# Loads of v and z on another queue, with casts on two engines, and two more blocks taken from their transposes

## The chip, the core and the metric

The kernel runs on one core of a Trainium2 chip. The metric is the device time of one execution in microseconds (us); lower is better. The core has TensorE (PE, matmuls), VectorE (DVE), ScalarE (ACT), GpSimd (POOL) and SyncE (SP), which here does nothing but issue transfers, and 16 DMA engines that move the data of all queues.

## What is computed

For each of 8 batches, with S = 3200 rows, D = 256, and z 64 wide:

```
scores = z @ z.T / S                       # symmetric, S x S
x      = u * (max(scores, 0)**2 @ v)       # S x D
q, k   = x @ w_q, x @ w_k                  # S x 64
mixed  = (q @ k.T / 8) @ x                 # done as q @ (k.T @ x)
out    = max(mixed, 0) @ w_out             # float32
```

Inputs and output are float32; the kernel's matmuls run in float16, but for a few at the end.

## The kernel before

The 3200 rows of a batch are 25 row tiles of 128. Columns are worked on in seven groups, six of 512 and one of 128 (`widths`, `starts`; `LASTG` is the last). One *score tile* is (batch, group gi, row tile ti): 128 rows by the group's columns.

*First product.* `scores` makes two score tiles at once (a pair), one on each half of PE's rows, line L263. `first_stage` takes max(., 0) and scales into a tile `g`, on ACT (L286) or DVE (L290). `second_stage` squares `g` into a float16 tile `at`, on ACT (L306) or POOL (L308). There are 16 buffers of `at` (`NAT`) and 7 of `g`.

*Turned blocks.* The scores are symmetric, so the block (gi, gj) transposed is the block (gj, gi). Where `is_turned` says so (gi < gj, and gj at most `FAR` = 2 groups on or the last group), the second one is not computed: `turn` sends the first one's `at` tiles through a transposing transfer of SP's queue (L330) into one of `NHOME` = 7 homes (`tt`, or `ttl` for the last group). Batch 0 leaves one such block out (`SKIP`).

*Second product.* For each group, `second_product` (L351) accumulates `at` (or `tt`, `ttl`) times `v` over the 25 row tiles in PSUM (`acc`), in two halves. `gate` takes the result out (L368, L369) and multiplies it by u into x on POOL (L388).

*The token part.* x is transposed by SP's queue (L400), projected to q and k (L417), the keys are transposed by SP's queue (L436) and doubled on POOL (L448), k.T @ x is summed up (L455, L470), and after the last group of a batch the mixing (L483) and the output projection (L521) run in the next batch's time, with stores on SP's queue (L552).

*v and z of the next batch.* `load_v` (L150) and `load_z` (L156) are transfers of POOL's queue that convert float32 to float16 on the way: z in one, v in five of 5 row tiles. `turn_z` (L163) then transposes z by SP's queue into `zT`. u is loaded by SP's queue (L174) as float32.

*The order of the work* is fixed when the program is written, by a planner that keeps a clock for each engine, and for SP's queue and the DMA engines (`sp_at`, `dma_at`). `move(ready, due, issue, takes, fn, landed, may)` registers a transfer of SP's queue; `send` issues the one that is due first once it is ready and calls `landed` with the time at which the data is reckoned to be there. `at_time` runs something at a time. `use_pair` makes a pair of score tiles, `squares` places second stages, `acc_step` issues second products, `half_done` gates, `use_keys`, `use_heads`, `use_mix` and `use_projs` the token part. The plan's times only set the order; on the chip each instruction waits for what it really needs, and each engine and queue keeps its order.

Of the kernel before, what the change touches and what calls it, by code (L numbers as in the profile page):

```python
# [16 lines left out]
def kernel(  # L17
# [45 lines left out]
    pk = ctx.enter_context(tc.tile_pool(name="pk", bufs=3))  # L63
    pxt = ctx.enter_context(tc.tile_pool(name="pxt", bufs=NXT))
    pu = ctx.enter_context(tc.tile_pool(name="pu", bufs=2))
    pg = ctx.enter_context(tc.tile_pool(name="pg", bufs=7))
    psum = ctx.enter_context(tc.tile_pool(name="psum", bufs=3))
    pat = ctx.enter_context(tc.tile_pool(name="pat", bufs=NAT))
    ptt = ctx.enter_context(tc.tile_pool(name="ptt", bufs=1))
# [20 lines left out]
    def rows(t, b):  # L90
        return t[b].rearrange("(p n) d -> p n d", n=NT)
# [52 lines left out]
            nc.tensor.matmul(out=idle[:, 0:P], lhsT=blank, rhs=blank, start=True, stop=True)  # L144
        clock[PE] += 0.053 * cold() * n

    def load_v(b, n0, nn):
        if n0 == 0:
            vs[b] = pv.tile([P, NT, D], FP16, tag="v_sb", name="v_sb")
        nc.gpsimd.dma_start(out=vs[b][:, n0 : n0 + nn, :], in_=rows(v, b)[:, n0 : n0 + nn, :])  # L150

    ztimes = []
    ZTURNS = [(0, 0, 7), (1, 0, 7), (0, 7, 13), (1, 7, 13)]

    def load_z(b):
        nc.gpsimd.dma_start(out=zn[:, 1 : NT + 1, :], in_=rows(z, b))  # L156

    def turn_z(b, i):
        odd, m0, m1 = ZTURNS[i]
# [48 lines left out]


    SKIP = [(0, 2)]  # L210
    EXTRA = []

    def is_turned(b, gi, gj):
        if b == 0 and (gi, gj) in SKIP:
# [392 lines left out]
    moves = []  # L607
    sp_at, dma_at = [0.0], [0.0]
    LANDS = 4.0
    RING = 2.0  # L610
    SLACK = 1.0

    def at_time(t, fn):
        later.append((t, fn))

    def move(ready, due, issue, takes, fn, landed=None, may=None):
        moves.append((ready, due, issue, takes, fn, landed, may))

# [36 lines left out]

    FARDUE = 12.0
    SPLIT = 0.2
    UNTIL = 24.0

    def choose(a, d):  # L660
        t = shut() + LATE
# [33 lines left out]
    def squares():  # L695
        while pending and pending[0][0] <= clock[PE] + 0.3:
            ready, p, g = pending.pop(0)
            a, c = max(clock[ACT], ready), max(clock[POOL], ready)
            by_act = a + SPARE < c and (a + 1.06 <= shut() + LATE or a + 2.5 < c)
            ways = [by_act]  # L700
            if clock[PE] < UNTIL and max(a + 0.63, c + 1.05) + SPLIT < min(a + 1.06, c + 1.9):
                ways = [a < c, a >= c]
                done = max(give(ACT, ready, 0.63), give(POOL, ready, 1.05))
            else:
                done = give(ACT, ready, 1.06) if by_act else give(POOL, ready, 1.9)
            for (b, gi, gj, _, nn, _, _), turn in second_stage(p, g, ways):
# [24 lines left out]

    def use_keys(b, gi):
        open_slot()
        ps = ps_tile("qk")
        prior = None
        if keyed and keys_at.get(keyed[0], 1e9) <= clock[PE]:
            prior = keyed.pop(0)
        projections(b, gi, ps, stop=not prior)
        clock[PE] += 0.44 if gi < LASTG else 0.24
        if prior:  # L740
            heads(*prior, ps, halves(gi))
            clock[PE] += 0.44 if prior[1] < LASTG else 0.11
        ready = clock[PE] + FROM_PE
        a, d = (max(clock[x], ready) for x in (ACT, DVE))
        by_act = a + 0.58 <= d + 0.69 or d + 0.69 > shut() + LATE + 0.6
        projections_out(b, gi, ps, by_act)
        done = give(ACT, ready, 0.58) if by_act else give(DVE, ready, 0.69)
        n = widths[gi] / P
        final = (b, gi) == (last, LASTG - 2)
        if not final:  # L750
            move(
                done + SLACK, done + 10.0, 1.28, 0.21 * n, lambda: turn_keys(b, gi),
                lambda t: at_time(t, lambda: double(b, gi)),
            )
            keyed.append((b, gi))
        if prior:
            heads_out(*prior, ps)
            done = give(DVE, done, 0.7)
            if prior[1] == LASTG:
                give(POOL, done, 0.6)  # L760
                heads_known(prior[0])
        close_slot(done)
        if len(keyed) == 2 and gi == LASTG:
            add_extra(done + 14.0, "heads", use_heads)
        if final:
            for _ in keyed[1:]:
                add_extra(done, "heads", use_heads)
# [49 lines left out]
    def project_out(b, gi, ps, ready):  # L817
        stores = []
        on_act = max(clock[ACT], ready) + BIAS <= max(clock[DVE], ready) + 0.2
        proj_out(b, gi, ps, [(not on_act, nc.sync, widths[gi] // P)], stores)  # L820
        engine, t = (ACT, 1.0) if on_act else (DVE, 1.23)
        done = give(engine, ready, t if gi < LASTG else 0.3)
        close_slot(done)
        i = len(stored)
        if gi < LASTG:
            stored.append(1e9)

        def landed(t):
# [12 lines left out]
    V1 = 10  # L841

    def batch_begun(b, t):
        if b + 1 < B:
            t0 = max(t + 6, Z0)
            at_time(t0, lambda: (load_z(b + 1), push(3.0)))
            step = ZSTEP if b else ZSTEP0
            for i, (_, m0, m1) in enumerate(ZTURNS):
                move(
                    t0 + ZWAIT + step * i, t0 + ZDUE + step * i, 1.28, 0.21 * (m1 - m0),  # L850
                    lambda i=i: turn_z(b + 1, i),
                    lambda t, i=i: z_ready.update({(b + 1, i): t}),
                )
# [4 lines left out]
    def v_loaded(b, n0, nn):  # L858
        load_v(b, n0, nn)
        push(2.5)  # L860
        for n in range(n0, n0 + nn):
            v_at[b, n] = dma_at[0] + 5.0

    z_ready = {}

# [4 lines left out]
    def group_begun(b, gi, t):  # L870
        if gi == 0:
            batch_begun(b, t)
        if gi + 1 < NG:
            move(max(t + 2, clock[POOL] + SLACK), t + 7, 0.55, 1.6, lambda: load_u(b, gi + 1))
        elif b + 1 < B:
            move(max(t + 2, clock[POOL] + SLACK), t + 7, 0.55, 1.6, lambda: load_u(b + 1, 0))

    SPARE = 0.5
    BIAS = 0.2
    XDUE = 5.0  # L880
    XWAIT = 2.0
    LATE = 0.5

    def half_done(b, gi, half):
# [10 lines left out]
        if half == halves(gi)[-1]:  # L895
            n = 8 if widths[gi] == W else 2
            move(
                t + SLACK, t + XDUE, 1.28, 0.21 * n, lambda: turn_x(b, gi),
                lambda t: x_landed(t, b, gi), lambda: len(xTs) < NXT,
            )  # L900

# [119 lines left out]
    move(10.0, 14.0, 0.55, 1.6, lambda: load_u(0, 0))  # L1021
# [153 lines left out]
```

## Time and profile before

| | |
|---|---|
| median of 3 runs | 775.03 us (774.68 to 778.61) |
| profiled execution | 773.15 us, its span 770.9 us |
| granted TensorE clock in it | 0.997 |
| queue of SP (hardware) | 300224 packets, 123.13 MB |
| queue of POOL (software) | 6624 packets, 15.98 MB |
| score matmuls (L263) | 924 |
| second-product matmuls (L351) | 10000 |
| transposing transfers of tt / ttl / x / keys / z | 143 / 48 / 56 / 53 / 28 |

The span is what lies between the first and the last recorded instruction; the execution's own time is 2.25 us longer. Busy times are unions of an engine's instructions; a line such as L263 is a line of the kernel before. "A <- B" after a wait means that A waited and that B ended the wait.

### The profile page before, as it was taken

How to read it: one execution, taken by the hardware profiler on the slowest of the kernel's cores; microseconds unless marked ns; L12 is line 12 of the kernel's file. 1: busy time of each engine (PE TensorE's matmuls, PEld its weight loads, DVE VectorE, ACT ScalarE, POOL GpSimd, SP SyncE). 2: the span in 40 equal slices, each digit the busy share in tenths (PEclk: the TensorE clock that was granted, in tenths of full speed). 3: DMA queues.
4: the chain of work that ended last, by engine and by line, in shares of the span. 5: the costliest groups of instructions: out<-in, count | busy, mean ns of one | idle time of the engine just before them, and what ended most of it. 6: DMA issues, size and time to landing. Idle time of an engine off the chain costs nothing.

```text
span 770.9 us, 28221 instructions
## 1 busy us (share of the span) xinstructions
PE 761.7 (99%) x12408; PEld 678.4 (88%) x12408; DVE 510.5 (66%) x537; ACT 561.2 (73%) x647; POOL 591.1 (77%) x496
## 2 busy tenths in 40 slices
PE   8999999999999999999999999999999999999996
PEld 7889998888898888989889988998889989898884
DVE  6775876675787566765677756765667476675645
ACT  7785876778758678875788677877777676777734
POOL 8796788789687778666778687887878887888740
PEclk9999999999999999999999999999999999999998
DMA  8999999999999999999899999999999998979625
GB/s 199 130 187 182 167 204 173 160 212 194 194 162 189 194 209 190 182 213 203 153 190 162 188 231 163 219 145 160 262 156 192 184 190 211 201 143 203 152 84 191
DMA packets 307114, 141.09 MB, mean 183 GB/s; under 512 B 285744, under 2 KB 288432, under 8 KB 306992
## 3 DMA queue, kind: packets, MB, share of 16 engines
q1 hardware_dynamic: 300224, 123.13, 85.0%
q0 software_dynamic: 6624, 15.98, 14.8%
q8 instruction: 97, 1.59, 0.9%
q14 instruction: 25, 0.20, 0.1%
q10 hardware_dynamic: 144, 0.20, 0.1%
HBM read 59.64 MB, written 26.21 MB: 111 GB/s over the span
## 4 chain that ended last, share of the span: by engine, by line
PE 94%; POOL 2%; DVE 1%; DMA 1%; ACT 1%; issue 1%; POOLq 0%; SPq 0%; DVEq 0%; ACTq 0%
PE acc L351 68%; PE sc L263 13%; PE fo L521 6%; PE qk L417 3%; PE qk L455 2%; POOL at L308 2%; PE mx L483 1%; DMA z<-in_z_dram 1%; POOL x_sb L388 1%; DVE g L290 0%; ACT g L286 0%; DVE fo L546 0%; DMA xT_sb<-x_sb 0%; PE hd L455 0%; ACT at L306 0%
## 5 line engine op out<-in xcount | busy, mean ns | idle before, releaser
L351 PE MATMUL acc<-v_sb,at 64*128 64x256 f16 x7344 | 504.7, 269 | 0.0
L308 POOL TENSOR_TENSOR at<-g 128x1024 f16<-128x1024 f32 (+1 forms) x218 | 402.3, 1859 | 71.6 <-ACT g L286 29.1
L351 PEld LDWEIGHTS <-at 64*128 64x128 f16 x7344 | 407.2, 94 | 48.1 <-issue 4.8
L290 DVE TENSOR_SCALAR g<-sc 128x1024 f32<-128x1024 f32 (+2 forms) x285 | 338.5, 1203 | 122.8 <-PE sc L263 114.3
L306 ACT ACTIVATE at<-g 128x1024 f16<-128x1024 f32 (+2 forms) x255 | 257.2, 1023 | 21.8 <-DVE g L290 17.8
L286 ACT ACTIVATE g<-sc 128x1024 f32<-128x1024 f32 (+2 forms) x186 | 183.2, 989 | 76.8 <-PE sc L263 75.0
L388 POOL TENSOR_TENSOR x_sb<-both,u_sb 128x512 f16<-128x512 f32 (+1 forms) x112 | 135.8, 1217 | 81.6 <-DVE both L369 77.7
L263 PE MATMUL sc<-zT 64*128 64x512 f16 x924 | 188.1, 375 | 1.4 <-DVE g L290 0.6
L351 PE MATMUL acc<-v_sb,tt 64*128 64x256 f16 x2272 | 163.4, 269 | 0.0
L351 PEld LDWEIGHTS <-tt 64*128 64x128 f16 x2272 | 126.2, 94 | 10.3
L369 DVE TENSOR_TENSOR both<-acc,both 128x512 f32<-128x512 f32 (+1 forms) x104 | 69.6, 670 | 21.4 <-ACT both L368 17.0
L263 PEld LDWEIGHTS <-zT 64*128 64x128 f16 x924 | 61.2, 94 | 7.6 <-issue 3.9
L368 ACT COPY both<-acc 128x512 f32<-128x512 f32 (+1 forms) x69 | 39.0, 565 | 38.7 <-PE acc L351 36.1
L546 DVE TENSOR_SCALAR fo<-fo 128x1024 f32<-128x1024 f32 (+1 forms) x28 | 32.4, 1166 | 46.6 <-PE fo L521 46.6
L509 ACT ACTIVATE rt<-mx 128x1024 f16<-128x1024 f32 x39 | 39.9, 1024 | 12.6 <-PE mx L483 12.1
L521 PE MATMUL fo<-wo,rt 128*128 128x256 f16 x386 | 46.6, 273 | 0.5 <-ACT rt L505 0.5
L521 PEld LDWEIGHTS <-rt 128*128 128x128 f16 x386 | 36.2, 98 | 8.4 <-issue 3.6
L431 ACT CAST qk<-qk 128x512 f16<-128x512 f32 (+1 forms) x47 | 25.3, 539 | 24.6 <-PE qk L455 20.0
L368 DVE COPY both<-acc 128x512 f32<-128x512 f32 (+1 forms) x35 | 23.6, 674 | 21.2 <-PE acc L351 19.9
L470 DVE TENSOR_TENSOR ha<-qk,ha 128x512 f32<-128x512 f32 x37 | 25.5, 689 | 14.4 <-ACT qk L431 14.1
L551 ACT ACTIVATE fo<-fo 128x1024 f32<-128x1024 f32 (+2 forms) x23 | 22.5, 978 | 16.5 <-PE fo L521 15.8
L417 PE MATMUL qk<-xT_sb,wqk 64*128 64x256 f16 (+1 forms) x404 | 32.3, 265 | 0.0
(55 smaller groups left out, 282.9 us busy)
## 6 DMA issues: line engine op xcount, KB each, us to landing
u_sb<-in_u_dram SPq DMA_DIRECT2D x48, 512.0 KB, 4.8
out_dram<-fo SPq DMA_DIRECT2D x46, 512.0 KB, 5.1
v_sb<-in_v_dram POOLq DMA_DIRECT2D x35, 320.0 KB, 6.0
zn<-in_z_dram POOLq DMA_DIRECT2D x7, 400.0 KB, 7.8
tt<-at SPq DMA_TRANSPOSE x143, 4.7
u_sb<-in_u_dram SPq DMA_DIRECT2D x8, 128.0 KB, 2.9
out_dram<-fo SPq DMA_DIRECT2D x4, 256.0 KB, 3.3
xT_sb<-x_sb SPq DMA_TRANSPOSE x56, 5.4
```

The lines of the kernel that those rows point to most:

```text
L263: nc.tensor.matmul(out=sc[h][:, 0:gw] if banks else sc[:, h, 0:gw], lhsT=z_cols(b, h, ti * P, P), rhs=z_cols(b, h, gs, gw), start=True, st ...
L286: nc.scalar.activation(out=g[:, hs, 0:w], in_=part, func=RELU, scale=GSCALE)
L290: nc.vector.tensor_scalar(out=g[:, hs, 0:w], in0=part, scalar1=0.0, scalar2=GSCALE, op0=AOP.max, op1=AOP.mult,)
L306: nc.scalar.square(out=out, in_=g[:, hs, 0:w])
L308: nc.gpsimd.tensor_mul(out=out, in0=g[:, hs, 0:w], in1=g[:, hs, 0:w])
L351: nc.tensor.matmul(out=accs[half, r][:, ds((j % 2) * D, D)], lhsT=weights(b, gi, ti, j)[top(r), :], rhs=vs[b][top(r), ti, :], start=(first ...
L368: copy(out=both[:, 0 : n * D], in_=accs[half, 0][:, 0 : n * D])
L369: nc.vector.tensor_add(out=both[:, 0 : n * D], in0=accs[half, 1][:, 0 : n * D], in1=both[:, 0 : n * D])
L388: nc.gpsimd.tensor_mul(out=xs[b, gi][:, 0:n, :, r, :].rearrange("p n c d -> p (n c) d"), in0=both[:, 0 : n * D].rearrange("p (m d) -> p m ...
L417: nc.tensor.matmul(out=ps[:, r, 0 : n * P], lhsT=wqk[top(r), c, :, :].rearrange("p t h -> p (t h)"), rhs=xTs[b, gi][top(r), 0:n, c, :], st ...
L509: nc.scalar.activation(out=out, in_=part, func=RELU)
L521: nc.tensor.matmul(out=banks[r][:, ds(j * D, D)], lhsT=flat[:, ds((dc * n + j) * P, P)], rhs=wo[:, dc, :], start=(dc == 0 and j == 0), sto ...
```

## The change

Three things change.

1. *Loads.* z and v of the next batch are loaded by SP's queue as float32, in ten parts (`PARTS`: v or z, first row tile, number of them, place, and how many parts must be cast before). A part lands either in the not yet filled slots of the new `v_sb` buffer, read as float32, or in one of two staging tiles (`pst`). `cast_part` converts it, on ACT or POOL, into its place in `v_sb` or into `zn`, at most three row tiles of v or nine of z at a time. To make room, `g` has 6 buffers instead of 7.
2. *The plan.* The costs of transfers in `move` are changed (issue 1.28 to 1.25 and 0.55 to 0.45, `takes`, `RING`), the time from a landing to the place of what waits for it is raised (`TURNS` 3.5 instead of 0.5, `KEYS` 3, `STORES` 4 instead of 2, `XWAIT` 9 instead of 2, `CASTS` 6), and `lead` (how many steps of second product the score pairs may be ahead), `SPARE`, `BIAS` and `UNTIL` (which engine takes what) have other values.
3. *Blocks.* In batches 1 to 7 the blocks (0, 3) and (1, 4) are turned as well.

```diff
-    pg = ctx.enter_context(tc.tile_pool(name="pg", bufs=7))
+    pst = ctx.enter_context(tc.tile_pool(name="pst", bufs=1))
+    pg = ctx.enter_context(tc.tile_pool(name="pg", bufs=6))
...
-    def load_v(b, n0, nn):
-        if n0 == 0:
+    STAGES = (3, 2)
+    PARTS = [
+        (False, 0, 25, 12.5, 0),
+        (True, 0, 3, 6, 0),
+        (True, 3, 5, 15, 1),
+        (True, 8, 2, 11, 2),
+        (True, 10, 3, None, 0),
+        (True, 13, 2, None, 0),
+        (True, 15, 2, 21, 3),
+        (True, 17, 3, None, 5),
+        (True, 20, 2, None, 6),
+        (True, 22, 3, None, 8),
+    ]
+    stage_of = {}
+
+    def load_part(b, i):
+        is_v, n0, nn, slot, _ = PARTS[i]
+        if i == 0:
             vs[b] = pv.tile([P, NT, D], FP16, tag="v_sb", name="v_sb")
-        nc.gpsimd.dma_start(out=vs[b][:, n0 : n0 + nn, :], in_=rows(v, b)[:, n0 : n0 + nn, :])
+        size, what = (D, v) if is_v else (dqk, z)
+        if slot is None:
+            k = STAGES.index(nn)
+            stage = pst.tile([P, nn * D], FP32, tag=f"st{k}", name="st")[:]
+        else:
+            at = int(slot * D)
+            stage = vs[b][:].rearrange("p n d -> p (n d)")[:, at : at + 2 * nn * size].bitcast(FP32)
+        stage_of[b, i] = stage.rearrange("p (n d) -> p n d", d=size)
+        nc.sync.dma_start(out=stage_of[b, i], in_=rows(what, b)[:, n0 : n0 + nn, :])
+
+    def cast_part(b, i, m0, m1, by_act):
+        is_v, n0, _, _, _ = PARTS[i]
+        copy = nc.scalar.copy if by_act else nc.gpsimd.tensor_copy
+        out = vs[b][:, n0 + m0 : n0 + m1, :] if is_v else zn[:, 1 + m0 : 1 + m1, :]
+        copy(out=out, in_=stage_of[b, i][:, m0:m1, :])
...
-    def load_z(b):
-        nc.gpsimd.dma_start(out=zn[:, 1 : NT + 1, :], in_=rows(z, b))
...
-    EXTRA = []
+    EXTRA = [(0, 3), (1, 4)]
...
-    RING = 2.0
+    RING = 1.5
...
-        dma_at[0] = max(dma_at[0], begun) + takes
         sp_at[0] = max(begun + issue, dma_at[0] - RING)
+        dma_at[0] = max(dma_at[0], begun + max(issue, 0.9)) + takes
         if landed:
-            landed(max(sp_at[0], dma_at[0]) + LANDS)
+            landed(dma_at[0] + LANDS)
...
-    UNTIL = 24.0
+    UNTIL = 16.0
...
-                    done + SLACK, due + SLACK, 1.28, 0.21 * n, turn,
+                    done + SLACK, due + SLACK, 1.25, 0.2 + 0.13 * n, turn,
...
-                row_at[b, gj, starts[gi] // P + n] = t + 0.5
+                row_at[b, gj, starts[gi] // P + n] = t + TURNS
...
-                lambda t: at_time(t, lambda: double(b, gi)),
+                lambda t: at_time(t + KEYS, lambda: double(b, gi)),
...
-        move(done + SLACK, done + 6.0, 0.55, 1.6, stores[0], landed)
-
-    def push(takes):
-        give(POOL, clock[PE], 0.6)
-        dma_at[0] = max(dma_at[0], clock[PE]) + takes
+        move(done + SLACK, done + 6.0, 0.45, 1.7, stores[0], landed)
 
     Z0 = 24
-    ZWAIT, ZDUE, ZSTEP, ZSTEP0 = 14.0, 32.0, 7.0, 5.0
-    V0 = 56
-    V1 = 10
+    Z1 = 6
+    VTIMES = [0, 4, 18, 23, 28, 34, 40, 46, 53, 60]
+    V0 = 0.75
+    CASTS = 6.0
+    KEYS = 3.0
+    TURNS = 3.5
+    STORES = 4.0
+    ZWAIT, ZDUE, ZSTEP, ZSTEP0 = 1.0, 18.0, 7.0, 5.0
+    sent, cast = {}, {}
 
     def batch_begun(b, t):
...
-            at_time(t0, lambda: (load_z(b + 1), push(3.0)))
...
+        if b == 0:
+            nc.gpsimd.memset(zn[:, 0 : NT + 2 : NT + 1, :], 0.0)
+        t0 = max(t + Z1, Z0)
+        sent[b + 1], cast[b + 1] = 0, [0, 0.0]
+        for i, (is_v, _, nn, _, after) in enumerate(PARTS):
+            at = t0 + VTIMES[i] * (1.0 if b else V0)
+            move(
+                at, at + 8.0, 0.45, 0.2 + 1.5 * nn * (D if is_v else dqk) / 1024,
+                lambda i=i: part_sent(b + 1, i),
+                lambda t, i=i: at_time(t + CASTS, lambda: part_landed(b + 1, i)),
+                lambda i=i, after=after: sent[b + 1] == i and cast[b + 1][0] >= after
+                and (not after or cast[b + 1][1] + SLACK <= clock[PE]),
+            )
+
+    def part_sent(b, i):
+        sent[b] += 1
+        load_part(b, i)
+
+    def part_landed(b, i):
+        assert cast[b][0] == i
+        is_v, n0, nn, _, _ = PARTS[i]
+        size, most = (D, 3) if is_v else (dqk, 9)
+        for m0 in range(0, nn, most):
+            m1 = min(nn, m0 + most)
+            n = (m1 - m0) * size
+            a, c = (max(clock[x], clock[PE]) for x in (ACT, POOL))
+            t_act, t_pool = 0.19 + 0.00084 * n, 0.15 + 0.0009 * n
+            by_act = a + SPARE < c and (a + t_act <= shut() + LATE or a + 2.5 < c)
+            cast_part(b, i, m0, m1, by_act)
+            done = give(ACT, clock[PE], t_act) if by_act else give(POOL, clock[PE], t_pool)
+            if is_v:
+                v_at.update({(b, n0 + m): done + 0.3 for m in range(m0, m1)})
+        cast[b] = [i + 1, done]
+        if not is_v:
...
-            for i in range(5):
-                at = t + 20 + 13 * i if b else V0 + V1 * i
-                at_time(at, lambda i=i: v_loaded(b + 1, 5 * i, 5))
...
-    SPARE = 0.5
-    BIAS = 0.2
+    SPARE = 0.1
+    BIAS = 0.0
     XDUE = 5.0
-    XWAIT = 2.0
+    XWAIT = 9.0
...
-    lead = 140
+    lead = 180
...
-                and (x[1] != "proj" or all(t + 2.0 <= now for t in stored[-2:]))
+                and (x[1] != "proj" or all(t + STORES <= now for t in stored[-2:]))
```

The other calls of `move` get the same new costs. z's transposes (`turn_z`) are registered when the last z cast is placed, not when z's load is.

More of the change, by code (lines that the diff above doesn't have):

```diff
@@ L751, in use_keys @@
             move(
-                done + SLACK, done + 10.0, 1.28, 0.21 * n, lambda: turn_keys(b, gi),
-                lambda t: at_time(t, lambda: double(b, gi)),
+                done + SLACK, done + 10.0, 1.25, 0.2 + 0.13 * n, lambda: turn_keys(b, gi),
+                lambda t: at_time(t + KEYS, lambda: double(b, gi)),
             )
@@ new lines @@
+    VTIMES = [0, 4, 18, 23, 28, 34, 40, 46, 53, 60]
[6 more added lines that the diff above has]
+    sent, cast = {}, {}
+    def batch_begun(b, t):
+        if b + 1 == B:
+            return
+        if b == 0:
[11 more added lines that the diff above has]
+            )
@@ new lines, in part_sent @@
+    def part_sent(b, i):
[17 more added lines that the diff above has]
+        if not is_v:
+            step = ZSTEP if b > 1 else ZSTEP0
+            for k, (_, m0, m1) in enumerate(ZTURNS):
@@ L849, in batch_begun @@
                 move(
-                    t0 + ZWAIT + step * i, t0 + ZDUE + step * i, 1.28, 0.21 * (m1 - m0),
-                    lambda i=i: turn_z(b + 1, i),
-                    lambda t, i=i: z_ready.update({(b + 1, i): t}),
-                )
-            for i in range(5):
-                at = t + 20 + 13 * i if b else V0 + V1 * i
-                at_time(at, lambda i=i: v_loaded(b + 1, 5 * i, 5))
[L858 to L862, printed above, removed]
+                    done + ZWAIT + step * k, done + ZDUE + step * k, 1.25, 0.2 + 0.13 * (m1 - m0),
@@ L864 @@
+                    lambda k=k: turn_z(b, k),
+                    lambda t, k=k: z_ready.update({(b, k): t}),
+                )
     z_ready = {}
@@ L873, in group_begun @@
         if gi + 1 < NG:
-            move(max(t + 2, clock[POOL] + SLACK), t + 7, 0.55, 1.6, lambda: load_u(b, gi + 1))
+            move(max(t + 2, clock[POOL] + SLACK), t + 7, 0.45, 1.7, lambda: load_u(b, gi + 1))
         elif b + 1 < B:
-            move(max(t + 2, clock[POOL] + SLACK), t + 7, 0.55, 1.6, lambda: load_u(b + 1, 0))
-    SPARE = 0.5
-    BIAS = 0.2
+            move(max(t + 2, clock[POOL] + SLACK), t + 7, 0.45, 1.7, lambda: load_u(b + 1, 0))
+    SPARE = 0.1
+    BIAS = 0.0
     XDUE = 5.0
-    XWAIT = 2.0
+    XWAIT = 9.0
     LATE = 0.5
@@ L897, in half_done @@
             move(
-                t + SLACK, t + XDUE, 1.28, 0.21 * n, lambda: turn_x(b, gi),
+                t + SLACK, t + XDUE, 1.25, 0.2 + 0.13 * n, lambda: turn_x(b, gi),
                 lambda t: x_landed(t, b, gi), lambda: len(xTs) < NXT,
@@ L1020 @@
     at_time(V3, lambda: (load_first_v(4, 8), give(POOL, clock[PE], 0.6)))
-    move(10.0, 14.0, 0.55, 1.6, lambda: load_u(0, 0))
+    move(10.0, 14.0, 0.45, 1.7, lambda: load_u(0, 0))
     load_weights()
```

4 lines of the change are left out of this document (removed).

## The prediction

> **What bounds the kernel now.** I read the busy table first, then the busy time by stretches of the span, then what TensorE (PE) waited for, then the chain of work that ended last, and only then single instructions.
>
> ```profile
> PE 761.7 (99%) x12408; PEld 678.4 (88%) x12408; DVE 510.5 (66%) x537; ACT 561.2 (73%) x647; POOL 591.1 (77%) x496
> ```
>
> PE is busy for 99% of the span, the other engines for 66 to 77%. A share over the whole span hides stages, so next comes the view by stretches (length; busy time of PE, PEld, DVE, ACT, POOL; granted clock; DMA share; GB/s):
>
> ```profile
> 0.00:20.00 20.00, 18.05 (x232) 14.52 (x234) 13.46 (x17) 14.29 (x18) 16.59 (x21) 1.00 0.80 194
> 20.00:40.00 20.00, 19.84 (x331) 17.73 (x329) 14.71 (x16) 14.57 (x18) 15.61 (x11) 1.00 0.95 142
> 40.00:60.00 20.00, 19.42 (x314) 16.90 (x310) 15.29 (x15) 16.62 (x18) 18.85 (x18) 1.00 1.19 178
> 60.00:740.00 680.00, 679.89 (x11216) 610.33 (x11213) 451.91 (x472) 505.87 (x576) 534.87 (x445) 1.00 1.04 185
> 740.00:760.00 20.00, 19.63 (x290) 15.58 (x287) 9.77 (x16) 5.69 (x13) 5.18 (x4) 1.00 0.29 89
> 760.00:771.00 11.00, 4.91 (x44) 3.33 (x42) 5.40 (x5) 4.15 (x9) 0.00 (x0) 0.81 0.75 295
> ```
>
> From 60 to 740 us PE rests for 0.11 us in all. What it doesn't use lies in the first 60 us (1.95 + 0.16 + 0.58) and at the end. The waits of PE (waiter, what it waited for: us in total, times, longest) say the same, and the chain says who sets the pace:
>
> ```profile
> PE warm L144 <- DVE wo L996: 1.0, 1, 1.0
> PE sc L263 <- DVE g L290: 0.6, 2, 0.4
> ...
> by line: PE acc L351 68.3%; PE sc L263 12.7%; PE fo L521 5.8%; PE qk L417 2.8%; PE qk L455 2.4%; POOL at L308 1.6%; PE mx L483 1.4%; DMA z<-in_z_dram 0.6%; POOL x_sb L388 0.5%; issue 0.5%; DVE g L290 0.5%; ACT g L286 0.4%; DVE fo L546 0.3%;
> ```
>
> The PE lines named there make 93.4% of the span: each of those matmuls was released by the matmul before it. Nothing but less PE work shortens the stretch from 60 to 740; nothing but a new wait of PE lengthens it. Is a busy PE a fast one? The order of PE's instructions around 40 us shows it:
>
> ```profile
> 40.21 0.40 PE L263 MATMUL sc<-zT 64*128 64x512 f16 x2
> 40.42 1.16 PE L351 MATMUL acc<-v_sb,at 64*128 64x256 f16 x18
> 41.41 0.40 PE L263 MATMUL sc<-zT 64*128 64x512 f16 x2
> 41.62 1.16 PE L351 MATMUL acc<-v_sb,at 64*128 64x256 f16 x18
> ```
>
> Durations overlap, so the starts count. A pair of score matmuls takes 0.21 us of PE (40.21 to 40.42, 41.41 to 41.62), and 18 matmuls of the second product take 0.99 us (40.42 to 41.41), 0.055 us each, without a hole. The Trainium skill (Perfetto Trace Analysis, Identifying the Most-Contended Engine) warns that the matmul's busy share is a bad measure and the share of weight loads a better one; by its 88% a busy PE would still have 12% in reserve, and a smaller PE load need not show in the time. The starts above speak against that here; the case stands below as a rival.
>
> **Two more blocks turned.** In batches 1 to 7 the blocks (0,3) and (1,4), four score tiles of 128x512 each, are no longer computed a second time but taken from their transposes. A batch goes from 115 score tiles to 107, so 56 tiles, 28 pairs, fall away. (The count fits: 119 + 7 x 115 = 924, the number in the first row here.)
>
> ```profile
> L263 PE MATMUL sc<-zT 64*128 64x512 f16 x924 | 188.1, 375 | 1.4 <-DVE g L290 0.6 <-ACT g L286 0.3
> L290 DVE TENSOR_SCALAR g<-sc 128x1024 f32<-128x1024 f32 (+2 forms) x285 | 338.5, 1203 | 122.8 <-PE sc L263 114.3 <-POOL at L308 3.3 <-ACT g L286 1.8
> L286 ACT ACTIVATE g<-sc 128x1024 f32<-128x1024 f32 (+2 forms) x186 | 183.2, 989 | 76.8 <-PE sc L263 75.0 <-POOL kx L448 0.9 <-POOL hs L477 0.6
> L306 ACT ACTIVATE at<-g 128x1024 f16<-128x1024 f32 (+2 forms) x255 | 257.2, 1023 | 21.8 <-DVE g L290 17.8
> L308 POOL TENSOR_TENSOR at<-g 128x1024 f16<-128x1024 f32 (+1 forms) x218 | 402.3, 1859 | 71.6 <-ACT g L286 29.1 <-DVE g L290 29.0 <-issue 11.1
> L351 PE MATMUL acc<-v_sb,at 64*128 64x256 f16 x7344 | 504.7, 269 | 0.0
> L351 PE MATMUL acc<-v_sb,tt 64*128 64x256 f16 x2272 | 163.4, 269 | 0.0
> ```
>
> On PE that removes 28 x 0.21 = 5.9 us; the chain gives the same (12.7% of 770.9 us is 97.9 us for 924, 0.106 each, times 56 = 5.9). The second product keeps all its matmuls, and one that reads a turned block (tt) is no slower than one that reads at: 269 ns both. So **-5.9 us**, all of it in the stretch where PE is the bound. On the other engines a pair costs 0.989 + 1.023 us (both steps on ACT) up to 1.203 + 1.859 (DVE, then POOL): 56 to 86 us less over three engines.
>
> **Loads by SyncE, casts by engines.** The seven z loads and 35 v loads leave POOL's queue and become 70 plain fp32 loads on SP's; what the transfer converted is now converted by ACT or POOL: per batch 10 pieces of v and 3 of z, 8,000 elements a partition. Casts from SBUF of three sizes stand in the trace:
>
> ```profile
> L150 POOL DMA_DIRECT2D v_sb<-in_v_dram x35 | 20.7, 591 | 0.0
> L156 POOL DMA_DIRECT2D zn<-in_z_dram x7 | 4.1, 591 | 0.0
> ...
> L124 ACT CAST zd<-z 128x512 f16<-128x512 f32 x1 | 0.6, 619 | 1.8 <-DMA z<-in_z_dram 1.8
> L200 POOL CAST wo<-wo 128x512 f16<-128x512 f32 x1 | 0.6, 603 | 0.0
> L124 POOL CAST zd<-z 128x384 f16<-128x384 f32 x1 | 0.5, 503 | 1.4 <-DMA z<-in_z_dram 1.4
> L124 ACT CAST zd<-z 128x256 f16<-128x256 f32 x1 | 0.4, 404 | 1.2 <-DMA z<-in_z_dram 1.2
> ```
>
> On ACT that is 0.84 ns an element and 0.19 us a piece, on POOL 0.78 and 0.2: a batch costs 13 x 0.19 + 8,000 x 0.00084 = 9.2 us on ACT, 8.8 on POOL, so 62 to 64 us for seven. Against it stand 24.8 us of issue that POOL loses (20.7 + 4.1) and the 56 to 86 of the pairs: the three engines together get 17 to 49 us less to do, and they had 145 (POOL), 174 (ACT) and 228 us (DVE) idle between 60 and 740. Cost on the path there: nothing while no cast waits for its load, for behind a waiting cast on ACT or POOL stand squares, copies of acc and gates. The plan puts a cast 10 us (LANDS 4, CASTS 6) behind the end it reckons for the transfer. The nearest row (size, median us from issue to landing):
>
> ```profile
> v_sb<-in_v_dram POOLq DMA_DIRECT2D x35, 320.0 KB, 6.0
> ```
>
> (That is 320 KB as it lands in fp16, 640 KB as it is read.) A v part of the new kernel reads 256 to 640 KB, so some 6 us at most, inside the 10. I take 0.2 us for PE's waits in the middle, about its 0.6 us of waits on DVE before spread over less; bounds 0 and the third rival.
>
> **SyncE's queue.** It gains 28 transposes (the four tiles of a block go as two pairs) and 70 loads:
>
> ```profile
> L330 SPq DMA_TRANSPOSE tt<-at x143: 1231/1354/5576, 17.1 to 713.4; - x143
> 317.19 0.53 SPq L174 DMA_DIRECT2D u_sb<-in_u_dram  x1
> SPq L330 <- POOL at L308: 51.2, 37, 2.8
> SPq L330 <- ACT at L306: 48.7, 32, 5.4
> ...
> 299.56 2.04 SPq L436 DMA_TRANSPOSE kx<-qk  x1
> ...
> 319.80 6.75 SPq L330 DMA_TRANSPOSE tt<-at  x2
> ...
> 355.22 1.22 SPq L436 DMA_TRANSPOSE kx<-qk  x1
> ```
>
> With the median 1.354 us a transpose and 0.53 a load: 37.9 + 37.1 = 75 us more issue. The queue's two longest waits alone, both for at tiles that POOL or ACT had not made yet, are 99.9 us: over the whole span there is room. In stretches there is none: from 299.56 to past 355 the queue goes from one transfer to the next, and two transposes took 6.75 us instead of 2.7 because transfers ahead of them were not through. Behind a held SP stand u loads (gates wait for them), transposes of x and of keys, and stores. None of that waited long before, and the later places (blocks taken 3.5 us after their reckoned landing where it was 0.5, keys 3, projections 9 where it was 2, stores 4 where it was 2) move work on PE, ACT and POOL away from such waits. They issue nothing; the plan fills the gap with other rows, of which it now has more in hand: lead 180 instead of 140 steps lets scores run 15.6 pairs ahead instead of 12.9, with 16 buffers of at. I take 0, and keep the third rival for the rest. One buffer of g less (6) is covered by DVE's small wait for POOL's squares above (3.3 us in all).
>
> **The start.** In the first batch the casts come early. Between 37 and 55 us the plan has z (3 pieces, 1.9 us) and the first 8 rows of v (3 pieces, 2.3 us) converted, 4.2 us, and takes two issues of 0.59 us from POOL. There POOL is busy 18.85 of 20 us and PE already loses 0.58 us, so scores arrive a little later: 3 us over three engines is 1 us, and the squares may move to ACT sooner (SPARE 0.1). Bounds -1 (the new balance removes part of the 0.74 us lost from 20 to 60) and +4; I take **+0.6**. The tail from 740 us on has the same instructions: 0, bounds -1 and +1.
>
> **Sum.** The profiled execution took 773.15 us, its span 770.9. 773.15 - 5.9 + 0.6 + 0.2 = 768.05. The median of the runs is 775.03, 1.88 us above the profiled one, so on its scale **769.9 us**, 0.66% faster.
>
> **The rivals.**
> First, the start and the middle eat most of it: 4 us at the start, where POOL has only 1.15 us free from 40 to 60, and 0.3 us per batch from a cast that waits. -5.9 + 4 + 2 = 0, or half of it: 771 to 776. For it: POOL's 18.85 of 20. Against: DVE and ACT have 4.71 and 3.38 us free there.
>
> Second, PE's records hide waits, and taking matmuls away only uncovers them: 775. Against it: 0.055 us a matmul, start to start, and PE's 0.11 us of rest. It is where the Trainium skill's rule on weight loads above would lead.
>
> Third, slower: SP's queue becomes the bound. The 75 us are 10.7 us a batch; the solid stretch is 57 of a batch's 96 us (770.9 / 8), so 6.4 us of them fall where SP has no rest. Blocks that land late by this much overrun the 3 us that the plan adds for them, 3.4 us a batch; if PE finds other rows for half of it, 7 x 1.7 = 12 us: 782. It decides once the queue runs over 3 us behind the plan for a group's length. For it: the 6.75 us. Against: 99.9 us of waits for data, and no wait of PE on a transfer worth listing. The Trainium skill (Perfetto Trace Analysis, What "DMA-bound" means) says that a kernel is bound by the issuing engine once its track is solid DMA work; by that rule the stretch after 299 us is at its bound already and 782 is the result.
>
> Fourth, more: the retuned balance (BIAS, SPARE, UNTIL, the loads' places) also saves 2 us at the start: 767.
>
> **How the numbers follow.** Forecast 0.58, first rival 0.15, second 0.04, third 0.15, fourth 0.08. About 0.5%, 3.9 us, is what a measurement of this kernel can tell from no change: faster means below 771.2. The forecast's own range is 768.5 to 772, a tenth of its chance above 771.2; so faster is 0.52 + 0.08 + 0.02 of the first rival = 0.62. Same is 0.06 + 0.12 + 0.04 = 0.22; slower 0.16, the third rival and the rim of the first. The range 766.5 to 778 holds the forecast, both middle rivals and most of the fourth.
>
> **What would show it.** Right: 868 score matmuls at L263, 0.106 us each in the chain; PE's rest from 60 to 735 us below 1 us; 171 tt transposes; z and v in SP's list; no cast that waits for its load for long. Wrong: PE waiting for squares or for a transposed block in the middle of batches; rows "POOL or ACT cast <- DMA" of several us; PE's lost time in the first 60 us above 4 us.

## The result: slower, 801.2 us

The changed kernel takes 801.17 us (median of 6, 797.91 to 804.73) against 775.06 us before: a ratio of 1.0326, interval 1.0291 to 1.0362. The forecast was 769.9 us, the range to 778; the third rival had the direction, with 782. The profiled execution took 801.93 us, span 800.0.

First the view by stretches of the kernel after (the same columns as before):

```profile
0.00:60.00 60.00, 55.97 (x844) 48.96 (x846) 41.93 (x45) 46.24 (x55) 50.19 (x47) 0.97 0.87 174
60.00:740.00 680.00, 656.00 (x10723) 573.38 (x10720) 431.81 (x450) 478.67 (x562) 495.87 (x420) 0.99 1.08 209
740.00:780.00 40.00, 40.00 (x670) 34.93 (x665) 20.23 (x27) 15.12 (x20) 23.68 (x20) 1.00 0.60 133
780.00:800.00 20.00, 13.75 (x128) 9.58 (x126) 9.39 (x13) 10.49 (x20) 1.65 (x2) 0.94 0.67 236
```

From 60 to 740 us PE rests for 24.0 us where it rested for 0.11. The start (4.03 us of rest, 2.69 before) and the end changed little. ACT, DVE and POOL are all less busy than before, in the middle and over the whole span (1625.3 us for the three, 1662.8 before), as the sum of their work said; they are not what is short. The waits and the chain say what is (waiter, what it waited for: us in total, times, longest; lines of the changed kernel: L476 doubles the keys, L181 is the cast, L291 the scores, L379 the second product):

```profile
POOL kx L476 <- DMA kx<-qk: 61.7, 24, 6.4
...
ACT v_sb L181 <- DMA st<-in_v_dram: 11.6, 5, 3.8
POOL v_sb L181 <- DMA st<-in_v_dram: 11.2, 6, 4.1
...
ACT v_sb L181 <- DMA v_sb<-in_v_dram: 8.3, 5, 3.3
...
POOL v_sb L181 <- DMA v_sb<-in_v_dram: 2.0, 3, 0.9
```

```profile
PE 76%; DMA 9%; issue 4%; POOL 3%; ACT 3%; DVE 2%; SPq 1%; POOLq 0%; ACTq 0%; DVEq 0%
```

Before, PE's matmuls released one another for 93% of the span; now PE makes 76% and transfers 9%. Copies of keys waited 61.7 us for their transposes and casts of v 33.1 us for their loads, both on engines that keep their order. One such place, in time order on SP, ACT and PE:

```profile
138.34 0.53 SPq L175 DMA_DIRECT2D v_sb<-in_v_dram  x1
138.96 1.23 SPq L358 DMA_TRANSPOSE tt<-at  x1
140.25 0.57 SPq L175 DMA_DIRECT2D v_sb<-in_v_dram  x1
140.93 2.29 SPq L358 DMA_TRANSPOSE tt<-at  x1
```

```profile
139.08 1.03 ACT L314 ACTIVATE g<-sc 128x1024 f32<-128x1024 f32 x1
143.44 0.83 ACT L181 CAST v_sb<-v_sb 128x768 f16<-128x768 f32 x1 [3.33 <-DMA v_sb<-in_v_dram]
144.18 0.58 ACT L396 COPY both<-acc 128x512 f32<-128x512 f32 x1
144.66 1.03 ACT L314 ACTIVATE g<-sc 128x1024 f32<-128x1024 f32 x1
```

```profile
142.11 0.93 PE L379 MATMUL acc<-v_sb,tt 64*128 64x256 f16 x14
145.73 0.61 PE L291 MATMUL sc<-zT 64*128 64x512 f16 x2 [2.70 <-ACT g L314]
146.11 0.45 PE L379 MATMUL acc<-v_sb,tt 64*128 64x256 f16 x2
```

SP issued the v part (640 KB) at 138.34, and ACT could cast it 5.1 us later. ACT had that cast next in its order and stood 3.33 us for it; behind the cast stood the copy of acc and the first stage of scores, and PE rested 2.70 us. PE's busy time falls to 16.0 to 17.6 us of 20 in the stretches from 240, 360, 460 and 560 us as well: about once in a batch.

### The profile page after: what moved, and what is told of

The parts are those of the page before. It is cut to its first block, busy times and chain, and to the rows that moved or that the text cites. A ratio compares the mean times of both kernels' runs of the same rounds, so it can differ in the third digit from the quotient of the medians.

```text
span 800.0 us, 28288 instructions
## 1 busy us (share of the span) xinstructions
PE 765.7 (96%) x12352; PEld 666.9 (83%) x12352; DVE 503.4 (63%) x532; ACT 550.5 (69%) x655; POOL 571.4 (71%) x488
## 3 DMA queue, kind: packets, MB, share of 16 engines
q1 hardware_dynamic: 339872, 159.15, 100.6%
## 4 chain that ended last, share of the span: by engine, by line
PE 76%; DMA 9%; issue 4%; POOL 3%; ACT 3%; DVE 2%; SPq 1%; POOLq 0%; ACTq 0%; DVEq 0%
PE acc L379 55%; PE sc L291 10%; PE fo L549 5%; POOL at L336 2%; DMA st<-in_v_dram 2%; DMA kx<-qk 2%; PE qk L445 2%; PE qk L483 2%; DMA xT_sb<-x_sb 2%; DVE g L318 1%; ACT at L334 1%; PE mx L511 1%; DMA v_sb<-in_v_dram 1%; DMA z<-in_z_dram 1%; ACT g L314 1%
## 5 line engine op out<-in xcount | busy, mean ns | idle before, releaser
L379 PE MATMUL acc<-v_sb,at 64*128 64x256 f16 x6896 | 474.8, 272 | 2.1 <-POOL at L336 1.7
L336 POOL TENSOR_TENSOR at<-g 128x1024 f16<-128x1024 f32 (+2 forms) x205 | 375.8, 1842 | 77.7 <-DVE g L318 64.2
L379 PEld LDWEIGHTS <-at 64*128 64x128 f16 x6896 | 374.3, 95 | 57.4 <-issue 6.3
L334 ACT ACTIVATE at<-g 128x1024 f16<-128x1024 f32 (+2 forms) x241 | 241.5, 1024 | 39.5 <-DVE g L318 33.4
L291 PE MATMUL sc<-zT 64*128 64x512 f16 (+1 forms) x868 | 182.6, 379 | 12.0 <-ACT g L314 5.5
L379 PE MATMUL acc<-v_sb,tt 64*128 64x256 f16 x2720 | 192.5, 270 | 0.0
L314 ACT ACTIVATE g<-sc 128x1024 f32<-128x1024 f32 (+2 forms) x152 | 149.4, 989 | 53.8 <-PE sc L291 52.6
L379 PEld LDWEIGHTS <-tt 64*128 64x128 f16 x2720 | 150.0, 94 | 13.7
L291 PEld LDWEIGHTS <-zT 64*128 64x128 f16 x868 | 56.5, 95 | 18.1 <-issue 12.3
L476 POOL COPY kx<-kx 128x128 f16<-128x128 f16 (+1 forms) x99 | 25.7, 288 | 61.9 <-DMA kx<-qk 61.7
L579 ACT ACTIVATE fo<-fo 128x1024 f32<-128x1024 f32 (+2 forms) x43 | 40.9, 996 | 18.1 <-PE fo L549 16.2
```

Of the source, the lines that this page charges most:

```text
L291: nc.tensor.matmul(out=sc[h][:, 0:gw] if banks else sc[:, h, 0:gw], lhsT=z_cols(b, h, ti * P, P), rhs=z_cols(b, h, gs, gw), start=True, st ...
L314: nc.scalar.activation(out=g[:, hs, 0:w], in_=part, func=RELU, scale=GSCALE)
L334: nc.scalar.square(out=out, in_=g[:, hs, 0:w])
L336: nc.gpsimd.tensor_mul(out=out, in0=g[:, hs, 0:w], in1=g[:, hs, 0:w])
L379: nc.tensor.matmul(out=accs[half, r][:, ds((j % 2) * D, D)], lhsT=weights(b, gi, ti, j)[top(r), :], rhs=vs[b][top(r), ti, :], start=(first ...
L579: nc.scalar.mul(out=flat_out[:, sl], in_=part, mul=FINAL_SCALE)
```

## The experiments

The theories: the *transfers* (SP's queue and the DMA engines behind it have no room for what the change adds), the *order* (the plan with its new values, or the fewer score tiles, put the work in a bad order), and the *casts* (their work on ACT and POOL). Where a time is followed by one number and two in brackets, they are the ratio and its 95% interval. Ratios are against the kernel before, on the same chip.

**Taking the change apart.** The blocks alone:

```diff
-    EXTRA = []
+    EXTRA = [(0, 3), (1, 4)]
```

> The kernel before with the two more blocks turned and nothing else. Queue theory (SyncE's queue can't pass 28 more transposes and 70 loads as fast as the plan has them, and casts and key copies on ACT and POOL wait in order behind it): 28 transposes at the 1.85 us that one took in the changed kernel are 52 us more for a queue that had 99.9 us of waits for at tiles, so most of the 5.9 us of PE comes through: 768 to 776. Plan theory (the new costs, later places, lead and balance put the work in a bad order; blocks and loads do no harm): the full gain, 769. If the blocks themselves are the harm: above 785.

805.61 us, 1.0391 (1.0346 to 1.0435). The blocks alone cost at least as much as the whole change. PE's longest waits in this run are hardly for transfers:

```profile
PE sc L263 <- DVE g L290: 16.5, 25, 1.2
PE qk L417 <- DMA xT_sb<-x_sb: 3.5, 4, 1.3
```

Scores waited for the first stage to empty their PSUM; copies of keys waited 11.1 us for their transposes.

The changed kernel without them (`EXTRA = []`):

> The changed kernel without the two blocks: loads by SyncE, casts and the new plan stay. Queue theory: of the added 52 us of transposes and 41 us of loads on the queue the 52 go, so more than half of the 32 us of waits that PE gained goes, while PE gets 5.9 us more work: 785 to 792. Plan theory and cast theory (the 63 us of casts on ACT and POOL delay squares, whatever the queue does): the waits stay and PE has 5.9 us more: 805 to 808.

781.43 us, 1.0071 (1.0041 to 1.0100): most of the loss is gone, although PE has the score work back. So the casts' work, which is all still there, isn't the cause by itself.

The changed kernel with the loads of the kernel before (the load's line alone):

```diff
-        nc.sync.dma_start(out=stage_of[b, i], in_=...)   # and the casts
+        nc.gpsimd.dma_start(out=vs[b][:, n0 : n0 + nn, :], in_=...)
```

> The changed kernel with z and v loaded by POOL's queue as before (conversion in the transfer, no casts, 7 buffers of g); the two blocks and the new plan's costs, places, lead and balance stay. Queue theory: 41 us less on the queue, no casts that wait: 778 to 788, with key copies still waiting. Cast theory: all waits gone, 769 to 773. Plan theory: no better than 797.

789.59 us, 1.0181 (1.0134 to 1.0229). Beside the blocks the loads and casts, with the order that they bring, cost some 11 us; without them the copies of keys still wait 61.1 us. The new plan alone, without loads and blocks:

> The kernel before with the new plan alone: costs, later places, lead, balance; loads by POOL's queue and blocks as before. By the run without the two blocks (781.4 with loads and plan) the plan and the loads together cost 5.7 us; if the loads are the cost, 773 to 777; if the plan, 779 to 784.

780.93 us, 1.0060 (1.0019 to 1.0101). With the run without blocks (1.0071) it says that the loads cost nothing that can be seen where there are no added blocks, and that the plan's values cost about half a per cent.

**Is it the queue's issue?** The loads from another queue, one word changed each time:

```diff
-        nc.sync.dma_start(out=stage_of[b, i], ...
+        nc.gpsimd.dma_start(out=stage_of[b, i], ...   # or nc.scalar
```

> The changed kernel with one word changed: the 70 plain float32 loads are issued by POOL's queue instead of SyncE's; the casts by ACT and POOL, the two blocks and the plan stay. Queue theory: casts rarely wait for their loads, key copies wait less: 780 to 792 (POOL pays 70 x 0.59 = 41 us of issue). Cast theory and plan theory: 800 or more, since casts and places are the same.

> The changed kernel with the 70 loads of z and v issued by ACT's queue instead of SyncE's; casts, blocks and plan stay. If SyncE's issue is what is full: 41 us leave it, 778 to 790 although ACT pays some 0.5 us a load. If the DMA engines are full, the same bytes move: 798 to 815.

817.84 us, 1.0466 (1.0404 to 1.0528), and 816.27 us, 1.0496 (1.0441 to 1.0552). Taking 70 loads off SP's queue helps nothing. It isn't a clean test of the issue, though: ACT and POOL now issue them themselves and in their order. With ACT, an issue took 0.33 us at the median, but PE waited 16.9 us for four copies of acc, up to 9.5 us each; in front of the longest of these, at 64.62 us, ACT had a load that went out only at 64.21, 11 us after ACT's last work.

**What do the blocks do?** Less score work and more transposes, taken one at a time. Transposes without a use:

```diff
-    NHOME = 7
+    NHOME = 6
...
-            if is_turned(b, gi, gj):
+            if is_turned(b, gi, gj) or is_idle(b, gi, gj):     # (0,3), (1,4)
...
+            if is_idle(b, gi, gj):
+                spare = ptt.tile([P, 2, 4, P], FP16, tag="ttx", name="ttx", bufs=2)
+                out = spare[:].rearrange("p n j t -> p (n j) t")
+                nc.sync.dma_start_transpose(out=out[:, 0 : 4 * nn, :], in_=at[:, c0:c1])
+                return
...
+        if is_idle(b, gi, gj):
+            return
```

> The kernel before; the blocks (0,3) and (1,4) are still computed twice, but their at tiles are also sent through the transposing transfers, into a spare tile that nobody reads (one home less makes room; the plan does not use the seventh). PE, ACT, DVE and POOL have the work of the kernel before. Transfer theory (the queue and its DMA engines have no room for the added transposes): 790 to 808. Order theory (fewer score tiles in groups 3 and 4 ask for pairs earlier than the lead of 140 steps gives them, and the transfers are harmless): 775.

815.34 us, 1.0494 (1.0422 to 1.0566): 35 transposes (the tiles pair up less well here than the 28) cost 38 us without any change of the arithmetic, by the chip and by the order that the plan makes for them together. And the smaller score work without transposes:

```diff
-    EXTRA = []
+    EXTRA = [(0, 3), (1, 4)]
...
+        if b and (gj, gi) in EXTRA:
+            return ident
         return turned[b, gj, gi][:, j, ti - starts[gj] // P, :]
...
+                if b and (gi, gj) in EXTRA:
+                    out_of[p] = out_of.get(p, 0) + 1
+                    at_time(done + 8.0, lambda x=(p, b, gi, gj, nn): block_landed(clock[PE], *x))
+                    continue
...
-    lead = 140
+    lead = 180
```

> The kernel before without the second computation of the blocks (0,3) and (1,4), with lead 180, and without their transposes: the second product reads a constant tile in their place, so this leaves out the transposition of these blocks and those parts of the result are not the reference's. PE has 5.9 us less, the queue what it had. Transfer theory: the full gain, 767 to 772. Order theory: some of the loss stays, 775 to 790.

769.72 us, 0.9929 (0.9903 to 0.9954). PE's share of the forecast is there: -5.5 us (3.6 to 7.5 by the interval), where 5.9 was forecast. From 60 to 740 us this kernel's PE is busy for

```profile
60.00:740.00 680.00, 679.29 (x11226) 609.93 (x11224) 444.87 (x475) 462.23 (x518) 535.97 (x450) 1.00 1.08 186
```

The same in the changed kernel, with its loads, casts and plan:

> The changed kernel without the transposes of the blocks (0,3) and (1,4) on the queue or in the plan; the second product reads a constant tile in their place, so those parts of the result are not the reference's. Loads, casts and plan stay. If the added transposes are what breaks the changed kernel: 781.4 (loads and plan without blocks) less 5.9, 774 to 778. If loads and plan also lose by the smaller score work: 785 and more.

770.38 us, 0.9922 (0.9891 to 0.9952). Its stretch and its waits:

```profile
60.00:740.00 680.00, 678.90 (x11267) 605.34 (x11264) 445.71 (x468) 493.98 (x582) 512.33 (x433) 1.00 1.03 204
```

```profile
POOL kx L478 <- DMA kx<-qk: 9.4, 4, 3.5
...
POOL v_sb L181 <- DMA v_sb<-in_v_dram: 2.3, 1, 2.3
...
ACT v_sb L181 <- DMA st<-in_v_dram: 1.4, 1, 1.4
```

Without the 28 transposes the copies of keys wait 9.4 us instead of 61.7 and the casts a few instead of 33.1, with the same loads and the same values of the plan. The transposes are worth 801.2 - 770.4 = 31 us in the changed kernel, counting the order that the plan makes for them. Lead doesn't matter to that:

> The kernel before with the two blocks turned and lead 180 instead of 140. Transfer theory: the queue is as full as with lead 140, 795 to 806. Order theory: the gain comes through, 769 to 776.

806.22 us, 1.0389 (1.0298 to 1.0479), as with 140.

**The chip or the plan?** The plan reckons with every transfer, so an added one works twice: on the chip and in the order. From the kernel with the unused transposes, once only in the plan and once only on the chip:

```diff
-                nc.sync.dma_start_transpose(out=out[:, 0 : 4 * nn, :], in_=at[:, c0:c1])
                 return
```

> The run with the turned but unused blocks again, but the added transposes stand only in the plan: their place and cost on the queue are reckoned with and nothing is issued. If the chip's transfers are the harm: 775 to 782 (an order that reckons with a fuller queue than there is). If the order that the plan makes with dearer transfers is the harm: 805 to 815, as with the transposes issued.

```diff
-                    done + SLACK, due + SLACK, 1.28, 0.21 * n, turn,
+                    done + SLACK, due + SLACK, *((0.0, 0.0) if is_idle(b, gi, gj) else (1.28, 0.21 * n)), turn,
```

> The reverse: the added transposes are issued, but the plan reckons no cost for them, so the order is nearly that of the kernel before. If the chip's transfers are the harm: 790 to 815. If the plan's order is the harm: 775 to 780.

809.82 us, 1.0401 (1.0364 to 1.0437), and 806.68 us, 1.0354 (1.0307 to 1.0401). Each alone costs most of the 4.9% that both cost, so the two don't add up. The first of these runs has the order of the run with both, on ACT, DVE and POOL instruction for instruction: there the order alone is worth 4.0%, and sending the transposes adds 0.9%, with intervals that just overlap. The second has an order of its own, not quite that of the kernel before (ACT has 638 instructions instead of 647, DVE 545 instead of 537); the plan still holds an at buffer for the added transpose. No run has that order without the transfers, so its 3.5% need not all be the chip's.

In the order that reckons with transfers that don't exist, PE hardly waits for a transfer; from its timeline:

```profile
203.21 0.92 PE L268 MATMUL sc<-zT 64*128 64x512 f16 x4 [0.46 <-DVE g L295]
204.99 0.39 PE L268 MATMUL sc<-zT 64*128 64x512 f16 x2 [0.86 <-DVE g L295]
206.12 0.39 PE L268 MATMUL sc<-zT 64*128 64x512 f16 x2 [0.74 <-DVE g L295]
206.33 1.49 PE L358 MATMUL acc<-v_sb,at 64*128 64x256 f16 x24
```

Four times two score matmuls follow one another with no second product between them, and they wait for the first stage to empty their PSUM. That the plan put them there because it reckoned no row ready is my reading; the trace doesn't show it.

In the order that reckons no cost for transposes that do exist, the queue is late for everything else:

```profile
POOL kx L458 <- DMA kx<-qk: 25.9, 10, 5.1
...
PE qk L427 <- DMA xT_sb<-x_sb: 10.8, 7, 2.9
ACT at L311 <- DMA ttx<-at: 9.6, 3, 8.3
...
POOL at L313 <- DMA ttx<-at: 5.7, 2, 5.2
```

PE waits for transposes of x, POOL for those of keys, and squares for an at buffer that is still being turned.

The plan's cheaper costs in the changed kernel, set back:

> The changed kernel with the plan's old, dearer costs of transfers (1.28 and 0.21 a block column instead of 1.25 and 0.2 + 0.13; landing behind the later of queue and engines). If the cheaper costs are the harm (the plan believes the queue faster than it is, so casts and key copies come too early): 780 to 790. If the transfers are too many whatever is believed: 795 to 810.

796.74 us, 1.0251 (1.0213 to 1.0288). With the dearer costs the waits of key copies and casts mostly go, and most of the loss stays:

```profile
POOL kx L476 <- DMA kx<-qk: 10.4, 6, 4.2
...
PE sc L291 <- DVE g L318: 6.7, 14, 1.1
```

Copies of keys wait 10.4 us instead of 61.7 and no cast of v is listed as waiting for its load; but squares wait 17.1 us for at buffers that are still being turned, and PE's longest wait is the one of the order above. The cheaper costs decide where the loss shows, but are not the cause of most of it.

**Issue or data?** On the run that issues the transposes without planning them, so with its order, thin transposes and short stores:

```diff
-                nc.sync.dma_start_transpose(out=out[:, 0 : 4 * nn, :], in_=at[:, c0:c1])
+                nc.sync.dma_start_transpose(out=out[:, 0:1, :], in_=at[:, c0 : c0 + P])
```

> The run with the added transposes issued but not planned, each cut to its first 128 columns of at: as many issues on SyncE's queue, an eighth of the data or less. If SyncE's issue of a transfer is what there is no room for: 798 to 808 as with the whole ones. If the data behind the queue is: 775 to 785.

```diff
-                out=rows(out, b)[:, n0 + at : n0 + at + n, :],
-                in_=flat_out[:, sl].rearrange("p (n d) -> p n d", d=D),
+                out=rows(out, b)[:, n0 + at : n0 + at + 1, :],
+                in_=flat_out[:, sl].rearrange("p (n d) -> p n d", d=D)[:, 0:1, :],
```

> The run with the added transposes issued but not planned, and each store of the output sends one of its four row tiles (the other three are left out of the output); the plan knows nothing of either, so the order stays. If the DMA engines' data is what there is no room for: 775 to 788. If it is SyncE's issue: 800 to 808.

790.47 us, 1.0165 (1.0124 to 1.0206), and 793.31 us, 1.0179 (1.0116 to 1.0241). Both bring about half of the 3.5% back. The added transposes' rows (SP's time for one: min/median/max in ns), whole and thin:

```profile
L330 SPq DMA_TRANSPOSE ttx<-at x35: 1206/1300/3703, 104.8 to 721.3; - x35
```

```profile
L330 SPq DMA_TRANSPOSE ttx<-at x35: 1093/1222/2282, 104.2 to 704.2; - x35
```

So the data counts: with the same order on ACT, DVE, POOL and SP, less of it, of whichever transfer, brings half back. The other half isn't settled. A transpose of next to no data still holds SP for 1.22 us, 43 us for 35 of them; at buffers are held longer; and that order itself, without the transfers, was not run. Short stores on the kernel with blocks and lead 180:

> The kernel before with the two blocks turned and lead 180, and each store of the output sends one of its four row tiles (the other three are left out of the output): as many transfers on the queue, 3/4 of the stores' bytes less. If the DMA engines behind the queue are full (the stores' 26.2 MB go to under 8 MB, some 50 us of the engines' time by the 1.6 us that the plan reckons for 512 KB): 772 to 785. If SyncE's issue of each transfer is what is full: 798 to 806.

804.12 us, 1.0329 (1.0275 to 1.0382). This says little on the data: an order alone can cost as much, as the transposes that were planned and not issued show, and PE's longest wait here is again for the first stage (11.9 us in 21 waits), not for a transfer.

No version here beats the kernel before and computes everything.

## Why the prediction was wrong

*Two more blocks turned, -5.9 us:* right. Without the transposes it is 5.5 us (0.9929) and, with loads and plan, 6.1 us (0.9922 of 776.61).

*Loads by SyncE, casts by engines, nothing on the path while no cast waits:* the condition was right and the size of the casts' work too (blocks aside, the loads add nothing that can be seen to the plan's 0.6%). "Some 6 us at most" from issue to landing was nearly right too (medians of 3.5 to 6.0 us for the v parts, 6.9 for z). But "inside the 10" took that time from the issue, and the part was issued late: beside the added blocks casts waited 33.1 us.

*SyncE's queue, "I take 0":* this step failed; the term measured 31 us (801.2 less 770.4). The added issue itself was sized about right: summed over the trace, transfers hold SP for 699.5 us instead of 617.6, 82 more where 75 was forecast. What failed is the reason for the 0, that the later places move work away from waits and that "the plan fills the gap with other rows". On the chip, copies of keys and casts waited 94.8 us for transfers; and the order that the plan makes with more transposes costs 4.0% with none of them issued. How the 31 us divide between the two isn't settled.

I also read the 99.9 us of SP's waits for at tiles as room. That sum tells neither way. In the kernel after, with transfers late, the same two waits are

```profile
SPq L358 <- ACT at L334: 41.9, 24, 10.5
SPq L358 <- POOL at L336: 38.8, 33, 2.4
```

80.7 us; in the changed kernel without the added transposes, with the 70 loads on the queue and PE at rest for 1.1 us from 60 to 740, they are

```profile
SPq L358 <- POOL at L336: 38.7, 29, 3.6
SPq L358 <- ACT at L334: 38.0, 25, 9.8
```

76.7 us. A queue that keeps its order waits for the tile at its head and is late for all behind it, whether or not that costs anything. Nor would the share of the DMA engines have told. In the page of the kernel before it is (40 slices, busy share in tenths, then the share of 16 engines' time of SP's queue and POOL's)

```profile
DMA  8999999999999999999899999999999998979625
...
q1 hardware_dynamic: 300224, 123.13, 85.0%
q0 software_dynamic: 6624, 15.98, 14.8%
```

nine tenths or more in nearly every slice until the end, and 99.8% of the engines' time in two queues. In the changed kernel without the added transposes, which loses nothing, it is as full:

```profile
DMA  7899999999999999999999998999999999989326
...
q1 hardware_dynamic: 310304, 151.80, 97.9%
q0 software_dynamic: 576, 1.64, 1.1%
```

In the kernel after SP's queue alone stands at 100.6%, so the share isn't that of a limit. The transfers are no slower there either, at the median (us from issue to landing, before and after):

```profile
tt<-at SPq DMA_TRANSPOSE x143, 4.7
```

```profile
tt<-at SPq DMA_TRANSPOSE x171, 4.4
```

The key transposes that POOL waited for took 4.1 us at the median, all of them 3.9; POOL stood ready for most of those it waited for within 3 us of their issue. So what came late was mostly the issue, not the flight.

*The later places move work away from waits:* they didn't suffice on the chip with the blocks, and without the blocks the new plan cost 0.6%. Why it costs that with the full score work and nothing with the smaller isn't settled.

*The start, +0.6:* right in size: PE is busy 56.91 us of the first 60 in the changed kernel without transposes, 57.31 before; 55.97 in the kernel after, see the last section.

*The third rival* had the direction and the late transfers, but another place: it let turned blocks land late, and no wait of PE for one stands among the waits of the kernel after. What stood still were ACT and POOL, behind casts and key copies. Its price, 12 us, was too small. The Trainium skill's rule on solid issuing tracks (Perfetto Trace Analysis, What "DMA-bound" means) isn't shown to be behind the 24.0 us of rest: transfers hold SP for 699.5 of 800.0 us, and an order with no added transfer rests PE for 23.9 us in the same stretch (656.12 us busy of 680).

Of the second rival nothing was seen: without the added transposes, PE was done 5.5 us earlier with 5.9 us less to multiply.

## What to carry to other kernels

A term of a sum at 0 needs a reason that a run could refute. Here neither the queue's waits nor the share of the DMA engines told whether there was room, since both look the same in a kernel that loses nothing. Before costing work that is saved by a transfer, ask for the two halves by themselves: the saving without the transfer (here -5.5 us) and the transfer without the saving (here +38 us). Where a program orders the work beforehand, an added transfer acts twice, in the order and on the chip; a run that plans it and doesn't issue it shows what the order alone costs, here 4.0%.

## What the runs showed of the hardware

After some rests PE is slow for a while. Behind the 2.70 us of rest above, the granted clock (the figure after POOL's busy time) was 0.50 for some 3.4 us, and two score matmuls took 0.38 us (145.73 to 146.11) instead of 0.21:

```profile
145.00:146.00 1.00, 0.27 (x2) 0.13 (x3) 1.00 (x2) 1.00 (x2) 1.00 (x2) 0.83 1.28 287
146.00:147.00 1.00, 1.00 (x12) 0.74 (x10) 1.00 (x2) 1.00 (x2) 1.00 (x1) 0.50 0.75 165
...
149.00:150.00 1.00, 1.00 (x20) 0.87 (x18) 0.57 (x2) 0.04 (x1) 0.00 (x0) 0.96 1.10 183
```

From 60 to 740 us this happened four times in the kernel after, behind rests of 2.3 to 3.1 us, and not behind the others, of at most 1.8 us. The length of one rest doesn't decide alone: in the run with only the blocks, it happened behind one of 1.17 us. Four times 3.4 us at half the clock make 6.8 us of the loss, by estimate, beside 24.0 of rest. PE's busy time is no measure of it: it grew from 761.7 to 765.7 us here although 5.9 us of matmuls had gone, but also to 771.4 us in the run with transposes planned and not issued, where the granted clock was 1.00 from 60 to 740 us.

ACT and POOL wait for the first loads of z up to some 2 us longer in some executions than in others: 5.2 and 4.4 us in the run without transposes, 3.0 and 2.3 in the kernel before, and PE 2.4 us behind them in the former. In the profiled execution after they waited 4.9 and 4.1, in the changed kernel with the plan's old costs 3.1 and 2.1; so that part of its start isn't shown to be the change's.
